# Five filter taps per chunk, as whole rows read from the transposed bank, with the running sum in SBUF

## The chip, the cores and the metric

The kernel runs on one core of a Trainium2 chip. The metric is the device time of one execution in microseconds; each kernel is run several times and the median is given.

## What is computed

Attention with a decay that depends on the position, then a gated unit whose gate is a causal filter over five positions. Eight batches, eight heads, 576 positions, 64 per head; the heads side by side make 512 features.

```python
def _attn_ref(q, k, v, s):
    scores = scale * np.matmul(q, k.transpose(0, 1, 3, 2))
    cum = np.cumsum(np.maximum(s, 0.0), axis=-1)
    bias = -(cum[:, :, :, None] - cum[:, :, None, :])
    scores = np.where(causal, -1000000000.0, scores + np.minimum(bias, 0.0))
    ...
    return np.matmul(attn, v)

def _moe_ref(x, w_val, conv_w, w_out):
    xp = np.concatenate([np.zeros((B, K - 1, D)), x], axis=1)
    for k in range(K):
        gate_pre += conv_w[k][None, None, :] * xp[:, k:k + S, :]
    gate = 1.0 / (1.0 + np.exp(-gate_pre))
    val = x @ w_val
    return (gate * val @ w_out)
```

## The kernel before

The work is cut into 32 chunks, `n = 4 * b + p`: batch `b` and a pair `p` of heads, which is also a chunk of 128 of the 512 features. One chunk passes through these steps; the engine stands in brackets.

- q and k are loaded (issued by SP), cast to bf16 (POOL), transposed into a PSUM bank (PE, L529) and copied to `QKT` (ACT, L533). v is loaded and multiplied with the decay (POOL, L500).
- The scores of two heads go in three steps to one of two double banks `s` (PE, L538; the causal mask is added by the matmuls of L580), and ACT takes their exponentials into `P` (L583, 128 x 1024 each, three a chunk).
- `av`: the weighted sum of v, with the sum of the weights as a 65th column, one bank per head (PE, L593).
- `norm`: per head, a reciprocal (DVE, L599) and a product that writes the normalised x in bf16 to `xn` (DVE, L600).
- `x_T`: x is transposed by five PE transposes into a bank of 576 bf16 (L607), and `x_evac` copies that bank to `xT` in SBUF behind four zero columns (DVE, L611).
- `tap`: the filter. The row of 576 is done in two halves of 288. The first product, with the fifth weight, goes to a PSUM bank `gs`; it is made by ACT (L623) for the chunks in `ON_ACT` (21 of 32) and by DVE (L625) for the other 11. Four more taps on DVE (L629) multiply a shifted piece of `xT` by a weight per partition and add what the bank holds; three write the bank again and the last writes the sum to `gp` in SBUF.
- `tanh`: ACT turns `gp` into `th` (L633); the sigmoid of the reference is half of one plus the tanh of half the argument.
- `val`: x times w_val, two halves a chunk, four matmuls each into a bank (PE, L653), after all four chunks of the batch are in `xT`. `glu` multiplies with one plus `th` (DVE, L659).
- `out`: five blocks a batch, four matmuls each (PE, L665), copied to `ot` by ACT (L670) and stored (SP).

At the end DVE looks at the reciprocals (L810 to L812); if one is out of range, a slower general path runs, which it does not here.

PSUM has eight banks: the two double banks `s` take four, and four single banks `m` are shared by everything else: the transposed q and k, the two `av` of a chunk, the transposed x, the `gs` halves, `val` and `out`. `gp` has two buffers, `th` six, `P` three.

The order of the work is not written by hand. `Plan` holds a list of tasks, each with an engine, an assumed duration, a due time, the tasks it needs, and the buffers that it takes and gives back. `Plan.run` plays them out in time: each engine takes the ready task with the smallest due time, and the order that results is the order in which each engine's instructions are issued on the chip. Each engine runs its own list strictly in that order, so an instruction that waits holds up everything behind it. The due times come from the table `DUE` (in chunks, added to the chunk's number).

Of the kernel before, what the change touches and what calls it, by code (L numbers as in the profile page):

```python
# [16 lines left out]
B, H, S, D = 8, 8, 576, 64  # L17
DM = 512
NKB = 5
# [184 lines left out]
def pcol(kb, qb):  # L204
    if kb == qb:
        return kb * 128
    if qb == 4:
# [13 lines left out]

DUE = dict(av=0.35, norm=0.78, xt=0.86, xe=-3.88, tap=1.56, dtap=0.01, tanh=0.36, cpe=-12.17, val=4.61,
           dval=0.23, out=9.61, dout=0.77, oute=-13.36, qt=-3.41, qe=-3.11, tt=-2.05, te=-14.54, s4=-1.53,
           vp=-12.15, cast=-20.65, lqk=-9.83, lv=17.78)

ON_PE = ()
PE_CHUNK = 2

ON_ACT = tuple(n for n in range(32) if n % 3)


class Plan:
# [115 lines left out]
def main_path(ctx, tc, q, k, v, s, moe_w_val, moe_conv_w, moe_w_out, out, okcnt):  # L350
# [5 lines left out]
    nc = tc.nc  # L356
# [49 lines left out]
    xns = two("xn", [128, NKB, 512], BF16)  # L406
    xTs = two("xT", [128, 4, 4 + S], BF16)
# [5 lines left out]
    recs = one.tile([128, NS, 2, NKB], FP32, name="recs")  # L413
# [3 lines left out]
    cwT = one.tile([128, 4, 5], FP32, name="cwT")  # L417
# [17 lines left out]
    def decay_T():  # L435
        pt = bank("w", [128, NKB, 64])
        slot["w"] = pt
        for i in range(NKB):
            nc.tensor.transpose(pt[:, i, :], cum[:, WIN[i]:WIN[i] + 128], identf)

    t = add("DVE", 0.65, -8, relu, [t_s])
    t = add("DVE", 1.3, -8, total, [t])
    t = add("DVE", 0.75, -8, centre, [t])
    t = add("PE", 1.2, -8, decay_T, [t], take=[("m", "w")], mode="N")
    t_w = add("ACT", 0.5, -8, lambda: nc.scalar.activation(out=w, in_=slot["w"], func=AF.Exp), [t],
              give=[("m", "w")])
# [3 lines left out]
    for nm, src, dst, sc, key in (("wv", moe_w_val, wv, 1.0, -5), ("wo", moe_w_out, wo, 0.5, -2.4)):  # L450
# [3 lines left out]
        t = add("SP", 3.6, key, load, take=[("qkf", nm)])  # L454
# [27 lines left out]
    T = {}  # L482
# [110 lines left out]
                nc.tensor.matmul(ps[:, qb * 65:qb * 65 + 65], lhsT, Vps[b % 2][:, kb, 2 * p + hh, :],  # L593
                                 start=(kb == 0), stop=(kb == qb))

    def norm(n, hh):
        b, p = divmod(n, 4)
        pv = slot["av", n, hh].rearrange("t (g d) -> t g d", d=65)
        nc.vector.reciprocal(recs[:, n, hh], pv[:, :, 64])  # L599
        nc.vector.tensor_tensor(xns[b % 2][:, :, p * 128 + hh * 64:p * 128 + hh * 64 + 64], pv[:, :, 0:64],  # L600
                                recs[:, n, hh].unsqueeze(2).to_broadcast([128, NKB, 64]), ALU.mult)

    def x_T(n):
        b, p = divmod(n, 4)
        pt = slot["x", n] = bank(("x", n), [128, S], BF16)
        for i in (4, 0, 1, 2, 3):
            nc.tensor.transpose(pt[:, WIN[i]:WIN[i] + 128], xns[b % 2][:, i, p * 128:(p + 1) * 128], ident)  # L607

# [1 line left out]
        b, p = divmod(n, 4)  # L610
        nc.vector.tensor_copy(xTs[b % 2][:, p, 4:4 + S], slot["x", n])  # L611

    def tap(n, hf, m):

        b, c = divmod(n, 4)
        o = hf * 288
        xc = xTs[b % 2][:, c, o:o + 292]
        if m == 0:
            slot["gs", n, hf] = bank(("gs", n, hf), [128, 288])
            if hf == 0:  # L620
                slot["g", n] = work("gp", n, [128, S], FP32)
            if n in ON_ACT:
                nc.scalar.activation(out=slot["gs", n, hf], in_=xc[:, 4:292], func=AF.Copy, scale=cwT[:, c, 4:5])  # L623
            else:
                nc.vector.tensor_scalar(slot["gs", n, hf], xc[:, 4:292], cwT[:, c, 4:5], None, ALU.mult)  # L625
        else:
            gs = slot["gs", n, hf]
            dst = slot["g", n][:, o:o + 288] if m == 4 else gs
            nc.vector.scalar_tensor_tensor(dst, xc[:, m - 1:m + 287], cwT[:, c, m - 1:m], gs, ALU.mult, ALU.add)  # L629

    def tanh(n):
        th = slot["t", n] = work("th", n, [128, S], FP32)
# [42 lines left out]
    for b in range(B):  # L675
# [3 lines left out]
        if b == 0:  # L679
            t_tl = add("SP", 1.6, -8.4, lambda: load_tail(0))  # L680
            t_tail = T["tailc", 0] = add("DVE", 0.45, -6, lambda: nc.vector.tensor_copy(tailbs[0], tails[0]), [t_tl])
            for p in range(4):
                for wh in range(2):
# [3 lines left out]
                    t = add("SP", 0.95, -8.5 + 0.5 * p + wh * 0.01, ld)  # L687
                    T["cast", 0, wh, p] = add(("DVE", "ACT")[wh], (0.32, 0.5)[wh], p - 9, lambda p=p, wh=wh: cast_qk(
                        (nc.vector.tensor_copy, nc.scalar.copy)[wh], 0, wh, HP[p], slot["f", 0, wh, p]), [t])
                t = add("SP", 1.4, -8.3 + 0.5 * p, lambda p=p: load_v_pair(p))  # L690
                T["vp", 0, p] = add("DVE", 0.85, p - 2, lambda p=p: vprime(nc.vector, 0, p), [t, t_w])
        else:
            fs = []
            for wh in range(2):
                def ld(b=b, wh=wh):
                    f = slot["f", b, wh] = work("qkf", (b, wh), [128, 8, 256], FP32)
                    dma_qk(b, wh, slice(0, 8), f)
                t = add("SP", 3.8, n0 + DUE["lqk"], ld, take=[("qkf", (b, wh))])
# [10 lines left out]
            for p in range(4):  # L709
# [3 lines left out]
        t = T["tt", b] = add("PE", 0.25, n0 + DUE["tt"] if b else -6.5, lambda b=b: tail_T(b), [t_tail],  # L713
                             take=[("m", ("tt", b))], mode="N")
# [19 lines left out]
        for p in range(4):  # L734
            n = n0 + p
            es = []
            for i in range(3):
                take = [("s", ("s", n, i))] + ([("P", n)] if i == 0 else [])
                t = T["s", n, i] = add("PE", (0.56, 0.27, 0.27)[i], n + 0.3 * i, lambda n=n, i=i: scores(n, i),
                                       [T["qe", b, p], t_te, T.get(("s", n, i - 1)), T.get(("s", n - 1, 2))],  # L740
                                       take=take, mode="R")
                es.append(add("ACT", 0.905, n + 0.3 * i, lambda n=n, i=i: exps(n, i), [t],
                              give=[("s", ("s", n, i))]))
            ns = []
            for hh in range(2):
# [3 lines left out]
                ns.append(add("DVE", 0.62, n + DUE["norm"] + 0.1 * hh, lambda n=n, hh=hh: norm(n, hh),  # L749
                              [t, T.get(("xt", n - 8))], give=[("m", ("av", n, hh))]))  # L750
            T["norm", n] = ns[1]
            t = T["xt", n] = add("PE", 0.3, n + DUE["xt"], lambda n=n: x_T(n), ns, take=[("m", ("x", n))], mode="N")

            T["xe", n] = add("DVE", 0.37, n + DUE["xe"], lambda n=n: x_evac(n),
                             [t] + [T.get(("val", n0 - 8 + c, hf)) for c in range(4) for hf in range(2)]
                             + T.get(("conv", n - 8), []), give=[("m", ("x", n))])
            ths = []
            if PE_CONV(b, p):
                cs = []
                for hf in range(2):  # L760
                    t = add("PE", 1.85, n + DUE["cpe"], lambda n=n, hf=hf: conv_pe(n, hf), [T["xe", n], t_dg] + cs[-1:],
                            take=[("m", ("g", n, hf))], mode="N")
                    cs.append(t)
                    ths.append(add("ACT", 0.42, n + DUE["cpe"] + 0.2, lambda n=n, hf=hf: tanh_pe(n, hf), [t] + ths,
                                   take=[("th", n)] if hf == 0 else [], give=[("m", ("g", n, hf))]))
                T["conv", n] = cs
            else:
                ends = []
                for hf in range(2):
                    t = ends[0] if hf else None  # L770
                    for m in range(5):
                        take = [("gp", n)] if m + hf == 0 else []
                        if m == 0:
                            take = take + [("m", ("gs", n, hf))]
                        t = add("ACT" if m == 0 and n in ON_ACT else "DVE", 0.37, n + DUE["tap"] + (hf * 2.5 + m * 0.5) * DUE["dtap"],
                                lambda n=n, hf=hf, m=m: tap(n, hf, m), [T["xe", n], t_cw, t], take=take,
                                give=[("m", ("gs", n, hf))] if m == 4 else [])
                    ends.append(t)
                T["conv", n] = ends
# [102 lines left out]
```

## Time and profile before

| what | value |
|---|---|
| median of 3 runs | 270.92 us (270.29 to 271.18) |
| the profiled execution | 271.83 us |
| its span in the trace | 270.0 us |
| mean granted TensorE clock | 0.938 |
| busy: PE, DVE, ACT, POOL | 197.8, 226.0, 194.9, 73.3 us |
| DMA: moved, mean rate | 40.5 MB, 150 GB/s |

A group of instructions is written as its line, engine and operation, what it writes and reads by the program's names (buffer numbers left out), then partitions x elements and type, and after the bar the busy time in us, the mean duration of one in ns, the idle time of the engine just before such instructions and what ended it. So `L629 DVE ... m<-xT,cwT,m 128x288` is a tap of half a row. A row of the waits names who waited, for whom, the total in us, how often, and the longest. The 40 slices give the busy share in tenths. PE's busy time is that of overlapping matmuls and says less of how full PE is than it does for DVE and ACT.

### The profile page before, as it was taken

What the parts mean: (1) busy time and instruction counts of PE and PEld (TensorE: products, weight loads), DVE (VectorE), ACT (ScalarE), POOL (GpSimd) and SP (SyncE); (2) the same over time, 40 slices, a digit from 0 to 9 for tenths busy, and PEclk for the clock granted to TensorE, in tenths of its full rate; (3) what the DMA queues carried; (4) which work ended last, traced back from release to release, by engine and by line L of the source; (5) the groups of instructions that cost most, each with busy time, mean ns of one, the idle gap of its engine ahead of it and who ended that gap; (6) DMA issues with size and microseconds to landing.
All of it is one profiled execution on the core that took longest, in us unless ns stands there. A gap on an engine that the chain in (4) does not pass through costs nothing. (4 is left out here: it accounts for less than half of the span.)

```text
span 270.0 us, 6360 instructions
## 1 busy us (share of the span) xinstructions
PE 197.8 (73%) x2539; PEld 127.8 (47%) x2561; DVE 226.0 (84%) x524; ACT 194.9 (72%) x267; POOL 73.3 (27%) x73
## 2 busy tenths in 40 slices
PE   0788776766598679876849886887878776986660
PEld 0465642554456445553436553555445544543420
DVE  4453699899999898999987998999899999999920
ACT  2789788434888989878865787977987797684330
POOL 9204236457022810300930057042033000000000
PEclk9999965688889999999967999999999999999998
DMA  6999999989259970794421910752560120043133
GB/s 168 258 297 304 179 264 300 195 230 328 62 187 227 311 233 23 165 261 142 162 71 26 224 68 2 168 107 80 122 114 37 53 89 2 2 155 136 42 104 105
DMA packets 69232, 40.50 MB, mean 150 GB/s; under 512 B 47109, under 2 KB 63493, under 8 KB 69194
## 3 DMA queue, kind: packets, MB, share of 16 engines
q1 hardware_dynamic: 69194, 40.01, 56.7%
q8 instruction: 22, 0.36, 0.6%
q14 instruction: 16, 0.13, 0.2%
HBM read 30.57 MB, written 9.44 MB: 148 GB/s over the span
## 5 line engine op out<-in xcount | busy, mean ns | idle before, releaser
L583 ACT ACTIVATE P<-s 128x1024 bf16<-128x1024 f32 x96 | 95.1, 1027 | 14.4 <-PE s L580 9.5
L629 DVE SCALAR_TENSOR_TENSOR m<-xT,cwT,m 128x288 f32<-128x288 bf16 x192 | 99.6, 521 | 6.3 <-ACT m L623 1.6
L653 PE MATMUL m<-xT,wv 128*128 128x288 bf16 x256 | 43.6, 309 | 10.1 <-DVE gp L629 8.5
L538 PE MATMUL s<-QKT 64*128 64x128 bf16 (+4 forms) x576 | 41.4, 253 | 13.0 <-ACT P L583 10.6
L593 PE MATMUL m<-Vp,P 128*128 128x65 bf16 x960 | 40.8, 199 | 10.1 <-DVE gp L629 7.4
L500 POOL TENSOR_TENSOR Vp<-vst,w 128x650 bf16<-128x650 f32 x28 | 35.1, 1283 | 42.2 <-DMA vst<-in_v_dram 36.7
L665 PE MATMUL m<-wo,glu 128*128 128x512 bf16 x138 | 39.5, 384 | 9.5 <-DVE gp L629 7.3
L593 PEld LDWEIGHTS <-P 128*128 128x128 bf16 x960 | 36.4, 101 | 19.2 <-DVE gp L629 8.0
L538 PEld LDWEIGHTS <-QKT 64*128 64x128 bf16 x576 | 21.6, 99 | 34.0 <-issue 26.3
L533 ACT COPY QKT<-m 128x1024 bf16<-128x1024 bf16 x32 | 32.2, 1017 | 6.5 <-PE m L529 6.3
L653 PEld LDWEIGHTS <-wv 128*128 128x128 bf16 x256 | 24.6, 103 | 23.3 <-issue 13.6
L629 DVE SCALAR_TENSOR_TENSOR gp<-xT,cwT,m 128x288 f32<-128x288 bf16 x64 | 32.8, 514 | 2.1
L633 ACT ACTIVATE th<-gp 128x576 f32<-128x576 f32 x32 | 21.9, 684 | 15.9 <-DVE gp L629 15.6
L600 DVE TENSOR_TENSOR xn<-m,recs 128x320 bf16<-128x320 f32 x64 | 31.5, 492 | 2.2
L623 ACT ACTIVATE m<-xT,cwT 128x288 f32<-128x288 bf16 x42 | 21.1, 506 | 15.9 <-DVE glu L659 5.8
L670 ACT COPY ot<-m 128x512 f32<-128x512 f32 (+1 forms) x40 | 23.3, 584 | 11.9 <-PE m L665 9.4
L659 DVE SCALAR_TENSOR_TENSOR glu<-th,m 128x288 bf16<-128x288 f32 x64 | 26.7, 448 | 1.8 <-PE m L653 1.5
L665 PEld LDWEIGHTS <-glu 128*128 128x128 bf16 x160 | 14.4, 98 | 22.8 <-issue 7.5
L490 POOL CAST qb<-qkf 128x2048 bf16<-128x2048 f32 x7 | 13.3, 1894 | 37.1 <-issue 22.4
L529 PE MATMUL m<-ident,qb 128*128 128x128 bf16 x128 | 13.1, 227 | 12.0 <-DVE chalf L432 6.4
L607 PE MATMUL m<-ident,xn 128*128 128x128 bf16 x160 | 14.8, 225 | 6.4 <-DVE xn L600 5.1
L611 DVE COPY xT<-m 128x576 bf16<-128x576 bf16 x32 | 14.5, 452 | 4.4 <-PE m L607 4.3
(59 smaller groups left out, 160.2 us busy)
## 6 DMA issues: line engine op xcount, KB each, us to landing
out_dram<-ot SPq DMA_DIRECT2D x32, 256.0 KB, 2.1
qkf<-in_q_dram SPq DMA_DIRECT2D x7, 1024.0 KB, 5.9
qkf<-in_k_dram SPq DMA_DIRECT2D x7, 1024.0 KB, 7.9
vst<-in_v_dram SPq DMA_DIRECT2D x28, 256.0 KB, 5.0
vst<-in_v_dram SPq DMA_DIRECT2D x15, 128.0 KB, 4.3
first<-in_q_dram SPq DMA_DIRECT2D x4, 256.0 KB, 3.5
first<-in_k_dram SPq DMA_DIRECT2D x4, 256.0 KB, 3.6
tail<-in_q_dram SPq DMA_DIRECT2D x8, 128.0 KB, 8.8
```

What stands on the lines that cost most here:

```text
L500: eng.tensor_tensor(Vps[b % 2][:, :, h], vst[:, :, h], w[:, :, b * 8 + 2 * p:b * 8 + 2 * p + 2].unsqueeze(3).to_broadcast([128, NKB, 2, 65 ...
L533: nc.scalar.copy(QKTs[b % 2][:, :, p, 0:512].rearrange("d w (x j) -> d w x j", j=4), slot["qt", b, p].rearrange("d w (j x) -> d w x j", j=4))
L538: nc.tensor.matmul(ps[:, hh, c0:c0 + nq], QKTs[b % 2][r, 1, p, k0:k0 + 128], QKTs[b % 2][r, 0, p, q0:q0 + nq], **kw)
L583: nc.scalar.activation(out=slot["Pt", n][:, :, step * 512:(step + 1) * 512], in_=slot["s", n, step], func=AF.Exp, scale=0.125)
L593: nc.tensor.matmul(ps[:, qb * 65:qb * 65 + 65], lhsT, Vps[b % 2][:, kb, 2 * p + hh, :], start=(kb == 0), stop=(kb == qb))
L600: nc.vector.tensor_tensor(xns[b % 2][:, :, p * 128 + hh * 64:p * 128 + hh * 64 + 64], pv[:, :, 0:64], recs[:, n, hh].unsqueeze(2).to_broad ...
L629: nc.vector.scalar_tensor_tensor(dst, xc[:, m - 1:m + 287], cwT[:, c, m - 1:m], gs, ALU.mult, ALU.add)
L633: nc.scalar.activation(out=th, in_=slot["g", n], func=AF.Tanh, scale=0.5)
L653: nc.tensor.matmul(ps, wv[:, dc, c * 128:(c + 1) * 128], xTs[b % 2][:, dc, 4 + o:4 + o + 288], start=(dc == 0), stop=(dc == 3))
L659: nc.vector.scalar_tensor_tensor(glus[b % 2][:, c, o], slot["t", n][:, o], 1.0, slot["v", n, hf], ALU.add, ALU.mult)
L665: nc.tensor.matmul(ps, glus[b % 2][:, c, WIN[i]:WIN[i] + 128], wo[:, c, :], start=(c == 0), stop=(c == 3))
L670: nc.scalar.copy(ot[r, :], slot["o", b, i][r, :])
```

## The change

- A chunk's taps run over the whole row of 576 instead of two halves. They read x from the PSUM bank into which it was transposed, not from `xT`. The shift by one to four positions is made by shortening: tap `sh` reads `x[:, 0:576 - sh]` and adds to `gp[:, sh:576]`, so the zero columns are not needed for it.
- The running sum stays in `gp` in SBUF from the first product to the last tap; the `gs` banks are gone.
- `x_evac` still copies x to `xT`, for `val`, and the first product comes after it. The bank of x is given back after the fourth tap, no longer after the copy. `gp` is taken by `x_T`, no longer by the first product.
- The first product is on ACT for the 16 odd chunks and on DVE for the 16 even ones.
- `norm` is one task for both heads: two reciprocals, then two products. It waits for both `av`.
- The assumed durations of these tasks and most entries of `DUE` differ, so the order moves on every engine.

```diff
-DUE = dict(av=0.35, norm=0.78, xt=0.86, xe=-3.88, tap=1.56, dtap=0.01, tanh=0.36, cpe=-12.17, val=4.61,
+DUE = dict(av=0.17, norm=-1.06, xt=0.72, xe=0.23, tap=1.91, dtap=0.12, tanh=-1.57, cpe=-14.16, val=4.61,
...
-           vp=-12.15, cast=-20.65, lqk=-9.83, lv=17.78)
+           vp=-14.19, cast=-23.73, lqk=-8.62, lv=14.96)
...
-ON_ACT = tuple(n for n in range(32) if n % 3)
+ON_ACT = tuple(range(1, 32, 2))
...
-    def norm(n, hh):
+    def norm(n):
         b, p = divmod(n, 4)
...
+        pvs = [slot["av", n, hh].rearrange("t (g d) -> t g d", d=65) for hh in range(2)]
+        for hh in range(2):
+            nc.vector.reciprocal(recs[:, n, hh], pvs[hh][:, :, 64])
+        for hh in range(2):
+            nc.vector.tensor_tensor(xns[b % 2][:, :, p * 128 + hh * 64:p * 128 + hh * 64 + 64], pvs[hh][:, :, 0:64],
+                                    recs[:, n, hh].unsqueeze(2).to_broadcast([128, NKB, 64]), ALU.mult)
...
         pt = slot["x", n] = bank(("x", n), [128, S], BF16)
+        if not PE_CONV(b, p):
+            slot["g", n] = work("gp", n, [128, S], FP32)
...
-    def tap(n, hf, m):
+    def tap(n, m):
...
+        x, gp = slot["x", n], slot["g", n]
+        sh = (4 - (m - 1)) % 5 if m else 0
         if m == 0:
...
             if n in ON_ACT:
-                nc.scalar.activation(out=slot["gs", n, hf], in_=xc[:, 4:292], func=AF.Copy, scale=cwT[:, c, 4:5])
+                nc.scalar.activation(out=gp, in_=x, func=AF.Copy, scale=cwT[:, c, 4:5])
             else:
-                nc.vector.tensor_scalar(slot["gs", n, hf], xc[:, 4:292], cwT[:, c, 4:5], None, ALU.mult)
+                nc.vector.tensor_scalar(gp, x, cwT[:, c, 4:5], None, ALU.mult)
         else:
...
+            nc.vector.scalar_tensor_tensor(gp[:, sh:S], x[:, 0:S - sh], cwT[:, c, 4 - sh:5 - sh], gp[:, sh:S],
+                                           ALU.mult, ALU.add)
...
+            ns = [add("DVE", 1.1, n + DUE["norm"], lambda n=n: norm(n), [t, T.get(("xt", n - 8))],
+                      give=[("m", ("av", n, hh)) for hh in range(2)])]
...
+            t = T["xt", n] = add("PE", 0.3, n + DUE["xt"], lambda n=n: x_T(n), ns,
+                                 take=[("m", ("x", n))] + ([] if on_pe else [("gp", n)]), mode="N")
...
+                t = T["xe", n]
+                for m in range(5):
+                    act = m == 0 and n in ON_ACT
+                    t = add("ACT" if act else "DVE", 0.54 if act else 0.67, n + DUE["tap"] + m * DUE["dtap"],
+                            lambda n=n, m=m: tap(n, m), [t_cw, t], give=[("m", ("x", n))] if m == 4 else [])
+                T["conv", n] = [t]
```

Two places in the order. The first is DVE in the middle of the program, at a chunk whose first product DVE makes. Names carry a number for each tile: `m_2650` is one use of a shared bank, `gp_2651` one use of a sum buffer, and x2 or x3 counts equal rows that follow each other. Before, with `m_2650` and `m_2692` the two halves of one chunk:

```order
239 L625 TENSOR_SCALAR m_2650<-xT_118,cwT 128x288
240 L629 SCALAR_TENSOR_TENSOR m_2650<-xT_118,cwT,m_2650 128x288 x3
241 L629 SCALAR_TENSOR_TENSOR gp_2651<-xT_118,cwT,m_2650 128x288
242 L611 COPY xT_118<-m_2678 128x576
243 L625 TENSOR_SCALAR m_2692<-xT_118,cwT 128x288
244 L629 SCALAR_TENSOR_TENSOR m_2692<-xT_118,cwT,m_2692 128x288 x3
245 L629 SCALAR_TENSOR_TENSOR gp_2651<-xT_118,cwT,m_2692 128x288
```

And now, at such a chunk of the changed kernel, where `m_2452` is the bank of x, with the norm that follows:

```order
226 L615 COPY xT_118<-m_2452 128x576
227 L626 TENSOR_SCALAR gp_2453<-m_2452,cwT 128x576
228 L628 SCALAR_TENSOR_TENSOR gp_2453<-m_2452,cwT,gp_2453 128x572
229 L628 SCALAR_TENSOR_TENSOR gp_2453<-m_2452,cwT,gp_2453 128x573
230 L628 SCALAR_TENSOR_TENSOR gp_2453<-m_2452,cwT,gp_2453 128x574
231 L628 SCALAR_TENSOR_TENSOR gp_2453<-m_2452,cwT,gp_2453 128x575
232 L600 RECIPROCAL recs<-m_2494 128x5
233 L600 RECIPROCAL recs<-m_2527 128x5
234 L602 TENSOR_TENSOR xn_116<-m_2494,recs 128x5x64
235 L602 TENSOR_TENSOR xn_116<-m_2527,recs 128x5x64
```

Ten instructions of half a row have become five of a row, the source is the bank of x itself, and the taps follow directly on the copy of that bank; the norm's two reciprocals stand together.

The second place is ACT, also in the middle, around first products and tanh. Before:

```order
121 L623 ACTIVATE m_2052<-xT_119,cwT 128x288
122 L583 ACTIVATE P_1998<-s_2014 128x2x512
123 L633 ACTIVATE th_2070<-gp_1936 128x576
124 L533 COPY QKT_112<-m_2043 128x2x512
125 L623 ACTIVATE m_2091<-xT_119,cwT 128x288
126 L583 ACTIVATE P_1998<-s_2056 128x2x512
```

And now:

```order
121 L633 ACTIVATE th_2088<-gp_1981 128x576
122 L533 COPY QKT_113<-m_2090 128x2x512
123 L624 ACTIVATE gp_2082<-m_2081,cwT 128x576
124 L583 ACTIVATE P_2107<-s_2106 128x2x512
125 L583 ACTIVATE P_2107<-s_2121 128x2x512
126 L583 ACTIVATE P_2107<-s_2135 128x2x512
127 L633 ACTIVATE th_2164<-gp_2082 128x576
```

Two half products per chunk, each with its own place in ACT's list, have become one whole product that reads the bank of x and writes the sum buffer; the three exponentials of the next scores stand behind it and ahead of its tanh.

More of the change, by code (lines that the diff above doesn't have):

```diff
@@ L220 @@
 NEG = -30000.0
-DUE = dict(av=0.35, norm=0.78, xt=0.86, xe=-3.88, tap=1.56, dtap=0.01, tanh=0.36, cpe=-12.17, val=4.61,
-           dval=0.23, out=9.61, dout=0.77, oute=-13.36, qt=-3.41, qe=-3.11, tt=-2.05, te=-14.54, s4=-1.53,
-           vp=-12.15, cast=-20.65, lqk=-9.83, lv=17.78)
+DUE = dict(av=0.17, norm=-1.06, xt=0.72, xe=0.23, tap=1.91, dtap=0.12, tanh=-1.57, cpe=-14.16, val=4.61,
+           dval=0.42, out=9.65, dout=0.73, oute=-18.67, qt=-4.54, qe=-7.61, tt=-1.92, te=-14.48, s4=-1.31,
+           vp=-14.19, cast=-23.73, lqk=-8.62, lv=14.96)
 ON_PE = ()
 PE_CHUNK = 2
-ON_ACT = tuple(n for n in range(32) if n % 3)
+ON_ACT = tuple(range(1, 32, 2))
 class Plan:
@@ L594, in av @@
                                  start=(kb == 0), stop=(kb == qb))
-    def norm(n, hh):
+    def norm(n):
         b, p = divmod(n, 4)
[L598 to L601, printed above, removed]
+        pvs = [slot["av", n, hh].rearrange("t (g d) -> t g d", d=65) for hh in range(2)]
[4 more added lines that the diff above has]
+                                    recs[:, n, hh].unsqueeze(2).to_broadcast([128, NKB, 64]), ALU.mult)
     def x_T(n):
@@ L611, in x_evac @@
         nc.vector.tensor_copy(xTs[b % 2][:, p, 4:4 + S], slot["x", n])
-    def tap(n, hf, m):
+    def tap(n, m):
         b, c = divmod(n, 4)
-        o = hf * 288
-        xc = xTs[b % 2][:, c, o:o + 292]
+        x, gp = slot["x", n], slot["g", n]
+        sh = (4 - (m - 1)) % 5 if m else 0
         if m == 0:
-            slot["gs", n, hf] = bank(("gs", n, hf), [128, 288])
-            if hf == 0:
-                slot["g", n] = work("gp", n, [128, S], FP32)
             if n in ON_ACT:
-                nc.scalar.activation(out=slot["gs", n, hf], in_=xc[:, 4:292], func=AF.Copy, scale=cwT[:, c, 4:5])
+                nc.scalar.activation(out=gp, in_=x, func=AF.Copy, scale=cwT[:, c, 4:5])
             else:
-                nc.vector.tensor_scalar(slot["gs", n, hf], xc[:, 4:292], cwT[:, c, 4:5], None, ALU.mult)
+                nc.vector.tensor_scalar(gp, x, cwT[:, c, 4:5], None, ALU.mult)
         else:
-            gs = slot["gs", n, hf]
-            dst = slot["g", n][:, o:o + 288] if m == 4 else gs
-            nc.vector.scalar_tensor_tensor(dst, xc[:, m - 1:m + 287], cwT[:, c, m - 1:m], gs, ALU.mult, ALU.add)
+            nc.vector.scalar_tensor_tensor(gp[:, sh:S], x[:, 0:S - sh], cwT[:, c, 4 - sh:5 - sh], gp[:, sh:S],
+                                           ALU.mult, ALU.add)
     def tanh(n):
@@ L748, in main_path @@
                                         give=[("P", n)] if hh else [], mode="N")
[L749 to L752, printed above, removed]
+            ns = [add("DVE", 1.1, n + DUE["norm"], lambda n=n: norm(n), [t, T.get(("xt", n - 8))],
+                      give=[("m", ("av", n, hh)) for hh in range(2)])]
+            T["norm", n] = ns[0]
+            on_pe = PE_CONV(b, p)
+            t = T["xt", n] = add("PE", 0.3, n + DUE["xt"], lambda n=n: x_T(n), ns,
+                                 take=[("m", ("x", n))] + ([] if on_pe else [("gp", n)]), mode="N")
             T["xe", n] = add("DVE", 0.37, n + DUE["xe"], lambda n=n: x_evac(n),
                              [t] + [T.get(("val", n0 - 8 + c, hf)) for c in range(4) for hf in range(2)]
-                             + T.get(("conv", n - 8), []), give=[("m", ("x", n))])
+                             + T.get(("conv", n - 8), []), give=[("m", ("x", n))] if on_pe else [])
             ths = []
@@ L767, in main_path @@
             else:
[L768 to L779, printed above, removed]
+                t = T["xe", n]
[4 more added lines that the diff above has]
+                T["conv", n] = [t]
                 ths = [add("ACT", 0.59, n + DUE["tanh"], lambda n=n: tanh(n), [t], take=[("th", n)], give=[("gp", n)])]
```

## The prediction

> **What bounds the kernel now.** I read the page's list of busy times and its 40 slices first, then the table of stretches, then the groups of instructions, then who waited for whom, last the timeline of DVE near the end. The list of busy times alone does not settle it: DVE leads, but PE and ACT are not far behind.
>
> ```profile
> PE 197.8 (73%) x2539; PEld 127.8 (47%) x2561; DVE 226.0 (84%) x524; ACT 194.9 (72%) x267; POOL 73.3 (27%) x73
> DVE  4453699899999898999987998999899999999920
> ```
>
> The slices show why 84% is too low a figure for DVE: the first four are half empty (loads and the first scores), the last two are empty (the last stores), and between them almost every slice is at 8 or 9 tenths. The table of stretches puts numbers to it; its columns are the stretch, its length, and the busy time of PE, of the weight loads, of DVE, ACT and POOL.
>
> ```profile
> 30.00:60.00 30.00, 21.11 (x258) 13.96 (x256) 26.70 (x57) 20.54 (x27) 13.79 (x12) 0.70 0.97 233
> 60.00:90.00 30.00, 23.49 (x289) 15.85 (x290) 27.78 (x66) 21.95 (x31) 10.93 (x8) 0.90 0.82 213
> 90.00:120.00 30.00, 23.31 (x338) 15.10 (x343) 28.10 (x67) 26.18 (x35) 8.22 (x7) 1.00 0.72 187
> 120.00:150.00 30.00, 22.21 (x284) 14.26 (x280) 26.31 (x61) 21.82 (x30) 8.70 (x6) 0.89 0.37 114
> 150.00:180.00 30.00, 24.00 (x323) 15.31 (x328) 27.77 (x67) 25.07 (x35) 10.10 (x8) 1.00 0.51 108
> 180.00:210.00 30.00, 24.27 (x338) 15.91 (x341) 28.28 (x68) 23.37 (x33) 9.21 (x8) 1.00 0.36 89
> 210.00:240.00 30.00, 24.18 (x322) 14.89 (x325) 28.78 (x71) 24.20 (x35) 0.00 (x0) 1.00 0.15 54
> 240.00:258.00 18.00, 11.75 (x92) 6.73 (x95) 17.19 (x40) 7.93 (x14) 0.00 (x0) 1.00 0.28 96
> ```
>
> From 30 to 258 us, 228 us in all, DVE is busy 210.9 us (the sum of its column): 92.5%. Its lowest stretch is 26.31 of 30, 88%. The 32 chunks take 228 / 32 = 7.1 us each in this body. Who waited says the same from the other side: what ACT and PE wait for is mostly DVE's taps.
>
> ```profile
> ACT th L633 <- DVE gp L629: 15.6, 23, 2.6
> PE m L653 <- DVE gp L629: 8.5, 10, 1.7
> PE m L593 <- DVE gp L629: 7.4, 10, 1.5
> PE m L665 <- DVE gp L629: 7.3, 8, 1.4
> ```
>
> The tanh waits 15.6 us for the sums, and PE waits 8.5 + 7.4 + 7.3 = 23.2 us, in L653, L593 and L665, for a bank that a last tap frees. So DVE's work in the body is what the time is made of, and the costliest part of that work is what the change rewrites.
>
> **The taps.** These groups carry the terms: elements per partition, count, then busy us and mean ns of one.
>
> ```profile
> L629 DVE SCALAR_TENSOR_TENSOR m<-xT,cwT,m 128x288 f32<-128x288 bf16 x192 | 99.6, 521 | 6.3 <-ACT m L623 1.6
> L629 DVE SCALAR_TENSOR_TENSOR gp<-xT,cwT,m 128x288 f32<-128x288 bf16 x64 | 32.8, 514 | 2.1
> L625 DVE TENSOR_SCALAR m<-xT,cwT 128x288 f32<-128x288 bf16 x22 | 11.4, 517 | 0.6
> L659 DVE SCALAR_TENSOR_TENSOR glu<-th,m 128x288 bf16<-128x288 f32 x64 | 26.7, 448 | 1.8 <-PE m L653 1.5
> L811 DVE SCALAR_TENSOR_TENSOR ok<-recs,ok 128x320 f32<-128x320 f32 x1 | 0.5, 492 | 0.0
> L500 DVE TENSOR_TENSOR Vp<-vst,w 128x650 bf16<-128x650 f32 x4 | 3.3, 833 | 4.1 <-DMA vst<-in_v_dram 2.9 <-ACT w L445 1.2
> L600 DVE TENSOR_TENSOR xn<-m,recs 128x320 bf16<-128x320 f32 x64 | 31.5, 492 | 2.2
> L611 DVE COPY xT<-m 128x576 bf16<-128x576 bf16 x32 | 14.5, 452 | 4.4 <-PE m L607 4.3
> ```
>
> An element's price on DVE, from two rows of one operation: (833 - 492) / (650 - 320) = 1.03 ns. Of the 514 ns of a tap of 288, about 297 are elements and 217 are paid however short the row is. The change makes 128 taps of 572 to 575 elements out of 256 of 288 (in the order of DVE, a chunk's ten instructions become five), so half of those fixed parts go. A new tap is 514 + 286 x 1.03 = 809 ns. No row shows one that reads PSUM, adds to SBUF and writes SBUF, so I bound it: from below by the gate product, which reads one operand in PSUM and one in SBUF and writes SBUF, 448 + 286 x 1.03 = 743 ns; from above by no saving at all, 2 x 521 = 1042 ns. I take 809, since the tap that already writes gp is the same operation with the same kind of scalar. A first product on DVE becomes 517 + 288 x 1.03 = 814 ns; its ends are 452 (the copy of x, the same bank read in the same length) and 2 x 517 = 1034.
>
> The source moves from SBUF to PSUM. The rows give no price to that: the gate product with an operand in PSUM takes 448 ns for 288 elements, the all-SBUF product of L811 492 for 320, which is 492 - 32 x 1.03 = 459 for 288. [...] I stay with the rows, in which PSUM is not the dearer source.
>
> What an instruction occupies is not its duration. The timeline of DVE, start and duration in us:
>
> ```profile
> 240.92 0.52 DVE L625 TENSOR_SCALAR m<-xT,cwT 128x288 f32<-128x288 bf16 x1
> 241.48 1.64 DVE L629 SCALAR_TENSOR_TENSOR m<-xT,cwT,m 128x288 f32<-128x288 bf16 x3
> 243.15 0.52 DVE L629 SCALAR_TENSOR_TENSOR gp<-xT,cwT,m 128x288 f32<-128x288 bf16 x1
> 243.58 0.19 DVE L599 RECIPROCAL recs<-m 128x5 f32<-128x5 f32 x1
> 243.81 0.49 DVE L600 TENSOR_TENSOR xn<-m,recs 128x320 bf16<-128x320 f32 x1
> 244.21 1.63 DVE L629 SCALAR_TENSOR_TENSOR m<-xT,cwT,m 128x288 f32<-128x288 bf16 x3
> ```
>
> Three dependent taps take 243.15 - 241.48 = 1.67 us, 0.557 each, 0.034 more than a duration; the last one, followed by unrelated work, gives way after 0.43, 0.085 before its end. Half a chunk is 2.10 us (241.48 to 243.58), with its first product on DVE 2.66. Before, 21 chunks cost 4.20 and 11 cost 5.32: a mean of 4.59 us. After, four dependent taps cost 3 x 0.843 + 0.724 = 3.25, with the first product 0.848 more; 16 chunks each: a mean of 3.68. Saved: 0.91 us a chunk.
>
> **The norm.** A reciprocal and its product take 0.63 us (243.58 to 244.21), 1.26 a chunk; the product starts 0.23 after the reciprocal, which it needs. With both reciprocals first, the second fills that gap: 0.23 + 0.40 + 0.40 = 1.03. The saving lies between nothing and 0.23; I take 0.2. Both now wait for the second half's AV matmuls, and behind them on DVE stand the copy of x and the taps; the cover is DVE's own queue of taps, and if it runs dry the wait is one AV, 0.61 us in a row of PE quoted below, which eats the saving.
>
> Together 0.91 + 0.2 = 1.1 us a chunk, 35 us over 32 chunks. With the ends of the tap: 1.36 + 0 to 0.23 at 743 ns, about nothing at 1042.
>
> **ScalarE.** The first product of fewer chunks, over a whole row:
>
> ```profile
> L623 ACT ACTIVATE m<-xT,cwT 128x288 f32<-128x288 bf16 x42 | 21.1, 506 | 15.9 <-DVE glu L659 5.8 <-DVE xT L611 4.7 <-DVE gp L629 2.6
> L583 ACT ACTIVATE P<-s 128x1024 bf16<-128x1024 f32 x96 | 95.1, 1027 | 14.4 <-PE s L580 9.5 <-PE s L538 4.8
> L558 ACT ACTIVATE P<-s 128x128 bf16<-128x128 f32 x4 | 1.2, 294 | 0.4 <-PE s L553 0.4
> L633 ACT ACTIVATE th<-gp 128x576 f32<-128x576 f32 x32 | 21.9, 684 | 15.9 <-DVE gp L629 15.6
> ```
>
> An element costs (1027 - 294) / 896 = 0.82 ns, so a row of 576 is 506 + 288 x 0.82 = 742 ns, with the tanh's 684 below and 2 x 506 = 1012 above. ACT goes from 21.1 to 16 x 0.742 = 11.9 us: 9 us less, 0.3 a chunk. It hides under DVE now and matters only where ACT becomes the longest.
>
> **What is late next.** In the table, 30 us hold 30 / 7.1 = 4.2 chunks: 4.6 us off DVE, 1.2 off ACT, nothing off PE. The longest engine of each stretch is then DVE 22.1, PE 23.5, ACT 25.0, PE 22.2, PE 24.0, PE 24.3, PE or DVE 24.2, and in the last, with 2.5 chunks, DVE 14.4: together 179.7 us. Divided by the share that this engine reaches, it gives the new body. DVE reached 92.5%, as the one bound; with three engines within some 2 us in most stretches each waits for the others more often, and I take the lowest share of any stretch, 88%: 204 us, 24 less than 228. The profiled execution took 271.8 us (span 270.0); 271.8 - 24 = 248. It lies 0.9 above the median of the runs, 270.9, so I forecast **247 us**. Head and tail I leave as they are: DVE is not what is late there.
>
> The due times also shift the loads on SP's queue against the chunks (q and k by 1.2 chunks, v by 2.8) and the casts on POOL. POOL is idle most of the span and gets no more work; the stretch from 30 to 60 is the one where the transfers stand at 0.97. If it does not shrink at all, it keeps 30 us where I count 22.1 / 0.88 = 25.1: 5 us, a result of 252, inside the forecast.
>
> **Rivals.** *DVE stays the one bound, at 92.5%.* 179.7 / 0.925 = 194, 34 us less: 237. For it: the freed waits of ACT and PE are waits for DVE. Against it: ACT's 25.0 and PE's 24 beside it. 17%, 234 to 241.
>
> *The long row saves little,* or the new waits take most of it. At 1042 ns DVE is left as it was, and a few us remain, 268; with the body at 82%, 219, it is 9 us, 262. For it: no row shows this operand mix. Against it: the fixed 217 ns in three rows. 15%, 257 to 269.
>
> *Slower: banks.* x stays in its bank from the transposition to the fourth tap, some 5 us alone and up to two chunks' DVE work when others come between; and x_T now also needs a gp buffer, so it stands at PE's head until the tanh two chunks earlier is over. With the AV, val, out and q/k matmuls queued behind it on PE, ACT's exponentials run out. Two x at once leave 2 of 4 banks for the rest. What those hold, from the timeline of PE and two groups of ACT:
>
> ```profile
> 201.77 0.65 PE L653 MATMUL m<-xT,wv 128*128 128x288 bf16 x4
> 202.26 0.61 PE L593 MATMUL m<-Vp,P 128*128 128x65 bf16 x15
> ...
> 208.59 1.03 PE L665 MATMUL m<-wo,glu 128*128 128x512 bf16 x4
> ...
> 211.58 0.40 PE L529 MATMUL m<-ident,qb 128*128 128x128 bf16 x4
> 211.81 0.39 PE L529 MATMUL m<-ident,kb 128*128 128x128 bf16 x4
> ```
> ```profile
> L533 ACT COPY QKT<-m 128x1024 bf16<-128x1024 bf16 x32 | 32.2, 1017 | 6.5 <-PE m L529 6.3
> L670 ACT COPY ot<-m 128x512 f32<-128x512 f32 x32 | 18.6, 585 | 8.1 <-PE m L665 7.1 <-DMA out_dram<-ot 0.8
> ```
>
> Per chunk, waits left out, I estimate two AV banks of about 1.9 us (two AV, a reciprocal, one or two products of 0.49), two val banks of 0.65 + 0.45, one q/k bank of 0.62 + 1.02, and 1.25 out banks of 1.03 + 0.59: 3.8 + 2.2 + 1.6 + 2.0 = 9.6 us, 4.8 on two banks. It decides when queueing lengthens that by half, to 7.25 us a chunk, 0.15 over today's 7.1: 32 x 0.15 = 5 us, 276. For it: PE's 23 us of waits for banks. Against it: the two half-row banks go, 2 x 2.1 us or more a chunk. [...] 9%.
>
> *No change,* the two effects balancing: 4%.
>
> **The numbers.** Forecast 55%, 242 to 256; the rivals as said. About 0.3%, 0.8 us, is what a measurement of this kernel can tell from no change. Faster 55 + 17 + 15 = 87%, same 4%, slower 9%. The range of 8 in 10 takes the forecast, most of the first rival and a half of the second: 235 to 261.
>
> **What would show it.** Taps of 572 to 575 elements near 0.81 us, 128 of them, 104 us where 132 stood; DVE busy near 190; first products on ACT near 0.74; DVE's share of the body below 92%, with PE or ACT at its side; PE's waits for a bank, freed by a tap, not above 23 us. I am wrong if a tap takes over 0.95 us, or if PE's waits grow past 50.

## The result, and the profile after

| | before | after |
|---|---|---|
| median | 271.05 us | 239.80 us (4 runs, 239.30 to 241.54) |
| ratio, with its 95% interval | | 0.886 (0.881 to 0.891) |
| span of the profiled execution | 270.0 us | 237.6 us |

A few executions of a kernel fall into a slower state, and every median here is that of the others. The changed kernel is 31 us faster. The forecast was 247 us, 24 faster. The measured time lies in the range, but outside the forecast's own case (242 to 256) and inside that of the first rival (234 to 241). The page of after, busy times and DVE's slices:

```profile
PE 190.1 (80%) x2561; PEld 124.4 (52%) x2561; DVE 193.1 (81%) x390; ACT 184.9 (78%) x241; POOL 73.5 (31%) x73
DVE  4435599999999796998784996999999999999800
```

DVE lost 226.0 - 193.1 = 32.9 us, the span 32.4. The same table of stretches as before; the body now ends at 227 us, with DVE's last instruction (its last gate product ends at 225.4):

```profile
30.00:60.00 30.00, 22.10 (x316) 15.31 (x317) 29.31 (x52) 24.52 (x30) 14.82 (x14) 0.94 0.96 250
60.00:90.00 30.00, 27.53 (x419) 18.63 (x418) 27.77 (x60) 29.45 (x39) 19.13 (x13) 1.00 0.96 261
90.00:120.00 30.00, 24.45 (x320) 16.77 (x318) 25.02 (x51) 22.92 (x31) 9.31 (x7) 0.94 0.79 212
120.00:150.00 30.00, 24.29 (x359) 16.13 (x359) 23.80 (x50) 23.44 (x31) 9.30 (x7) 1.00 0.33 85
150.00:180.00 30.00, 27.84 (x387) 18.30 (x386) 29.16 (x61) 27.12 (x36) 8.83 (x8) 1.00 0.61 130
180.00:210.00 30.00, 27.63 (x383) 17.20 (x382) 29.12 (x61) 26.75 (x35) 1.17 (x1) 1.00 0.14 50
210.00:227.00 17.00, 14.34 (x109) 8.00 (x107) 14.79 (x30) 7.58 (x13) 0.00 (x0) 1.00 0.32 117
```

Three of the stretches have DVE at 97% or more (29.1 to 29.3 of 30) and one has ACT at 98% (29.45). Of the stretches of 30 us, only the two in the middle, 90 to 150 us, have no engine above 25.0. DVE as a whole is busy 179.0 of the body's 197 us, 90.8%; the longest engine of each stretch, summed, 181.1: 91.9%.

The groups of the tap, of its first products and of the norm, in mean ns:

```profile
L628 DVE SCALAR_TENSOR_TENSOR gp<-m,cwT,gp 128x575 f32<-128x575 bf16 x32 | 26.0, 814 | 0.6
L628 DVE SCALAR_TENSOR_TENSOR gp<-m,cwT,gp 128x572 f32<-128x572 bf16 x32 | 25.9, 810 | 3.2 <-ACT gp L624 2.8
L626 DVE TENSOR_SCALAR gp<-m,cwT 128x576 f32<-128x576 bf16 x16 | 13.0, 810 | 0.0
L624 ACT ACTIVATE gp<-m,cwT 128x576 f32<-128x576 bf16 x16 | 12.1, 756 | 5.3 <-DVE xT L615 2.8 <-DVE cwT L478 2.4
L600 DVE RECIPROCAL recs<-m 128x5 f32<-128x5 f32 x64 | 9.2, 176 | 11.0 <-PE m L593 11.0
```

A tap takes 810 to 814 ns, where 809 was worked out; a first product 810 on DVE (814) and 756 on ACT (742). The timeline of DVE shows what they occupy:

```profile
207.75 0.81 DVE L628 SCALAR_TENSOR_TENSOR gp<-m,cwT,gp 128x572 f32<-128x572 bf16 x1
208.47 0.26 DVE L600 RECIPROCAL recs<-m 128x5 f32<-128x5 f32 x2
208.70 0.89 DVE L602 TENSOR_TENSOR xn<-m,recs 128x320 bf16<-128x320 f32 x2
209.50 1.66 DVE L628 SCALAR_TENSOR_TENSOR gp<-m,cwT,gp 128x573 f32<-128x573 bf16 x2
211.07 0.45 DVE L615 COPY xT<-m 128x576 bf16<-128x576 bf16 x1
```

The norm takes 209.50 - 208.47 = 1.03 us, as estimated (it is also the median of the 32 chunks); the tap ahead of it gives way after 0.72; two dependent taps take 1.57 until the copy. The waits:

```profile
DVE recs L600 <- PE m L593: 11.0, 14, 2.3
ACT th L633 <- DVE gp L628: 6.6, 10, 1.4
PE m L653 <- DVE glu L659: 5.5, 8, 1.3
DVE gp L628 <- ACT gp L624: 2.8, 5, 1.7
DVE xT L615 <- PE m L611: 2.6, 5, 0.8
PE m L529 <- DVE gp L628: 2.4, 3, 1.3
PE m L593 <- DVE gp L628: 1.2, 3, 0.6
PE m L665 <- DVE gp L628: 1.0, 2, 0.6
PE m L653 <- DVE gp L628: 0.8, 1, 0.8
```

The tanh's wait for the sums went from 15.6 to 6.6 us, and PE's waits for a bank that a tap frees, in L653, L593 and L665, from 23.2 to 3.0; the row of 2.4 in L529 was 3.1 before. Two waits grew: the norm's for AV on DVE, from 5.8 to 11.0 us, now that its reciprocals come behind both heads, and PE's in L653 for a gate product, from 0.5 to 5.5.

### The profile page after: what moved, and what is told of

Same layout as the page of the kernel before. It is cut to its first block, busy times and chain, and to the rows that moved or that the text cites. A ratio compares the mean times of both kernels' runs of the same rounds, so it can differ in the third digit from the quotient of the medians.

```text
span 237.6 us, 6221 instructions
## 1 busy us (share of the span) xinstructions
PE 190.1 (80%) x2561; PEld 124.4 (52%) x2561; DVE 193.1 (81%) x390; ACT 184.9 (78%) x241; POOL 73.5 (31%) x73
## 5 line engine op out<-in xcount | busy, mean ns | idle before, releaser
L628 DVE SCALAR_TENSOR_TENSOR gp<-m,cwT,gp 128x572 f32<-128x572 bf16 (+3 forms) x128 | 103.7, 812 | 5.1 <-ACT gp L624 2.8
L538 PE MATMUL s<-QKT 64*128 64x128 bf16 (+4 forms) x576 | 40.6, 247 | 10.0 <-ACT P L583 7.4
L653 PE MATMUL m<-xT,wv 128*128 128x288 bf16 x256 | 40.5, 293 | 7.7 <-DVE glu L659 5.5
L593 PE MATMUL m<-Vp,P 128*128 128x65 bf16 x960 | 39.3, 197 | 4.4 <-DVE gp L628 1.2
L665 PE MATMUL m<-wo,glu 128*128 128x512 bf16 x160 | 40.2, 380 | 2.2 <-DVE gp L628 1.0
L593 PEld LDWEIGHTS <-P 128*128 128x128 bf16 x960 | 35.0, 100 | 12.6 <-issue 3.6
L538 PEld LDWEIGHTS <-QKT 64*128 64x128 bf16 x576 | 20.6, 96 | 27.6 <-issue 18.9
L653 PEld LDWEIGHTS <-wv 128*128 128x128 bf16 x256 | 24.1, 99 | 20.6 <-issue 12.7
L659 DVE SCALAR_TENSOR_TENSOR glu<-th,m 128x288 bf16<-128x288 f32 x64 | 27.8, 448 | 5.1 <-PE m L653 4.8
L602 DVE TENSOR_TENSOR xn<-m,recs 128x320 bf16<-128x320 f32 x64 | 28.1, 481 | 0.0
L665 PEld LDWEIGHTS <-glu 128*128 128x128 bf16 x160 | 14.2, 98 | 15.5 <-issue 3.6
L529 PE MATMUL m<-ident,qb 128*128 128x128 bf16 x128 | 13.1, 228 | 11.3 <-DVE chalf L432 6.1
L600 DVE RECIPROCAL recs<-m 128x5 f32<-128x5 f32 x64 | 9.2, 176 | 11.0 <-PE m L593 11.0
L529 PEld LDWEIGHTS <-qb 128*128 128x128 bf16 x128 | 8.7, 101 | 16.6 <-issue 7.7
```

The source lines that it names most:

```text
L538: nc.tensor.matmul(ps[:, hh, c0:c0 + nq], QKTs[b % 2][r, 1, p, k0:k0 + 128], QKTs[b % 2][r, 0, p, q0:q0 + nq], **kw)
L628: nc.vector.scalar_tensor_tensor(gp[:, sh:S], x[:, 0:S - sh], cwT[:, c, 4 - sh:5 - sh], gp[:, sh:S], ALU.mult, ALU.add)
L653: nc.tensor.matmul(ps, wv[:, dc, c * 128:(c + 1) * 128], xTs[b % 2][:, dc, 4 + o:4 + o + 288], start=(dc == 0), stop=(dc == 3))
L659: nc.vector.scalar_tensor_tensor(glus[b % 2][:, c, o], slot["t", n][:, o], 1.0, slot["v", n, hf], ALU.add, ALU.mult)
L665: nc.tensor.matmul(ps, glus[b % 2][:, c, WIN[i]:WIN[i] + 128], wo[:, c, :], start=(c == 0), stop=(c == 3))
```

## The experiments

Each differs from the changed kernel by the edit shown, unless it says otherwise. The times are medians; the changed kernel stands at 239.8, the kernel before at 271.05 to 271.4 beside the various runs.

**The source of the taps.** `e1_src_sbuf_hold`:

```diff
-        x, gp = slot["x", n], slot["g", n]
+        x, gp = xTs[b % 2][:, c, 4:4 + S], slot["g", n]
+        if m == 4:
+            x = slot["x", n]
```

> The first product and three of the four taps read the copy of x in SBUF; the last tap still reads the bank, so the bank is held as long as in the changed kernel, and the order is the same. If the source has no price, as the rows of before say: taps of 0.81 us from either memory, 240 us within 1. [...]

Measured: 265.6 us, 26 slower than the changed kernel (ratio to the kernel before 0.977, 0.974 to 0.981). The expectation does not hold. The lines of the taps in this run, minimum, median and longest in ns; then DVE and POOL by time:

```profile
L630 DVE SCALAR_TENSOR_TENSOR gp<-xT,cwT,gp x96: 799/815/2324, 31.5 to 246.1; 128x572 f32<-128x572 bf16 x32, 128x573 f32<-128x573 bf16 x32, 128x574 f32<-128x574 bf16 x32
L630 DVE SCALAR_TENSOR_TENSOR gp<-m,cwT,gp x32: 803/816/818, 34.1 to 246.9; 128x575 f32<-128x575 bf16 x32
```
```profile
121.04 1.66 DVE L630 SCALAR_TENSOR_TENSOR gp<-xT,cwT,gp 128x573 f32<-128x573 bf16 x2
123.64 0.80 DVE L630 SCALAR_TENSOR_TENSOR gp<-m,cwT,gp 128x575 f32<-128x575 bf16 x1
127.81 5.82 DVE L630 SCALAR_TENSOR_TENSOR gp<-xT,cwT,gp 128x572 f32<-128x572 bf16 x3
134.57 0.81 DVE L630 SCALAR_TENSOR_TENSOR gp<-m,cwT,gp 128x575 f32<-128x575 bf16 x1
```
```profile
125.57 1.89 POOL L490 CAST qb<-qkf 128x2048 bf16<-128x2048 f32 x1 [4.34 <-issue]
127.41 2.12 POOL L490 CAST kb<-qkf 128x2048 bf16<-128x2048 f32 x1
129.49 6.52 POOL L500 TENSOR_TENSOR Vp<-vst,w 128x650 bf16<-128x650 f32 x4
```

Most taps take 0.81 us from either memory. But a tap with both operands in SBUF that meets a cast or a product of POOL takes up to 2.3 us: from 127.4 to 136 us POOL works, and three taps with xT and gp in SBUF take 5.82 us together. Of the 96, the 31 that overlap such a POOL instruction take 1.49 us in the mean and the other 65 take 0.811. The tap that reads the bank never takes more than 0.818, here as in the changed kernel. POOL is held up as well: its products take 1.51 us instead of 1.28. DVE's busy time rises to 214.0 us, 21 above after. So the source does matter, in a way that the prediction did not have: beside a cast or product of POOL, the taps with both operands in SBUF took 1.49 us, and those with x in the bank 0.818 at most.

The first products on DVE, which have a single tensor operand, were changed in e1 too, and their line shows something else that nobody expected:

```profile
L628 DVE TENSOR_SCALAR gp<-xT,cwT x16: 510/562/1600, 30.7 to 238.2; 128x576 f32<-128x576 bf16 x16
```

The eight of them that meet nothing of POOL take 0.52 us, where they take 0.81 from the bank; the eight that meet POOL take up to 1.60. For this instruction SBUF is the cheaper source, by 0.29 us, when POOL is idle.

`e2_src_sbuf_free` leaves out the lines `if m == 4` as well, so all four taps have both operands in SBUF.

> As e1, but the last tap reads SBUF too, so the bank of x is free once it is copied, in the same order of instructions. If holding the bank through the taps costs anything: faster than e1, by up to the 5 us that PE waits for taps in the changed kernel. If banks are not what PE lacks: the same as e1 within 1 us.

Measured: 268.7 us, 3 slower than e1, where the same or less was expected, with a fourth tap exposed. Freeing the bank earlier in the same order bought nothing that shows beside that; it could not be parted from the source here.

`e10_pool_writes`, from e2: from the second batch on POOL no longer reads v, q and k. The kernel leaves out the scaled v and the casts and writes constants of the same shapes in their place.

```diff
-        eng.tensor_tensor(Vps[b % 2][:, :, h], vst[:, :, h],
...
+        if b:
+            for i in range(2):
+                eng.memset(Vps[b % 2][:, :, h], 1.0)
+            return
...
+        if b:
+            nc.gpsimd.memset(qkbs[which][b % 2][:, :, :], 0.25)
+            return
```

> As e2 (taps read SBUF twice), but from the second batch on POOL only writes constants of the same shapes into Vp, qb and kb, instead of reading v, q and k; the scaled v and the casts are left out. If POOL's reads of SBUF are what holds up a tap with two SBUF operands: taps that meet POOL take 0.81 us as the others do, no tap above 0.9, and the time falls from 270 to 241 or less. If a second SBUF operand is dear by itself, or POOL's writes hold it up too: taps of 1.4 us where they meet POOL, 260 or more.

Measured: 242.8 us, 26 faster than e2, with the same DVE instructions and POOL busy as long as in the changed kernel (73.2 us). The taps:

```profile
L635 DVE SCALAR_TENSOR_TENSOR gp<-xT,cwT,gp x128: 803/814/1146, 31.0 to 224.8; 128x572 f32<-128x572 bf16 x32, 128x573 f32<-128x573 bf16 x32, 128x574 f32<-128x574 bf16 x32, 128x575 f32<-128x575 bf16 x32
L633 DVE TENSOR_SCALAR gp<-xT,cwT x16: 512/520/2002, 30.4 to 216.1; 128x576 f32<-128x576 bf16 x16
```

The long taps are gone. Only three of 128 are above 0.83 us, up to 1.15, and each of them meets a cast of the tail, the one thing that POOL still reads for. So what held up the taps in e1, 1.49 us against 0.811, went with POOL's reads: here, with the same two SBUF operands and POOL writing, the median is 0.814 and no tap is long beside a POOL instruction that only writes. The first products (second line) behave otherwise: four of the 16 take 1.07 to 2.00 us, and each of these meets a constant that POOL writes, so for these four writing alone was enough. That is 5 us of DVE over the undisturbed 0.52 each, and the time lies 2 us above the 241 that was expected.

In e10 the bank of x is given back as early as in e2, and it still is 3 us slower than the changed kernel. So no gain from freeing the bank early shows here either, though the long first products cost some of it.

**Halves.** `e3_halves`:

```diff
-            nc.vector.scalar_tensor_tensor(gp[:, sh:S], x[:, 0:S - sh], cwT[:, c, 4 - sh:5 - sh], gp[:, sh:S],
-                                           ALU.mult, ALU.add)
+            for o, e in ((sh, 288), (288, S)):
+                nc.vector.scalar_tensor_tensor(gp[:, o:e], x[:, o - sh:e - sh], cwT[:, c, 4 - sh:5 - sh], gp[:, o:e],
+                                               ALU.mult, ALU.add)
...
+                for o in (0, 288):
+                    nc.vector.tensor_scalar(gp[:, o:o + 288], x[:, o:o + 288], cwT[:, c, 4:5], None, ALU.mult)
```

> Every tap and first product of DVE is cut into two halves again, still from the bank and with the sum in SBUF, in the same places of the order. Leaves nothing out. If each instruction simply pays its fixed 217 ns again: 8 x 0.557 against 3.25 us of taps a chunk, 1.2 us a chunk more, up to 38 us, near 275. If most of that is the wait of a tap for the one that it needs, which two halves taken in turn hide from each other: 8 x 0.43 = 3.44 us a chunk, 0.2 more, 6 us, 246.

Measured: 249.9 us (0.921, 0.916 to 0.926), 10 slower than whole rows. DVE is busy 205.2 us, 12 more, in this line of its page:

```profile
PE 191.5 (77%) x2561; PEld 125.1 (50%) x2561; DVE 205.2 (83%) x534; ACT 185.7 (75%) x241; POOL 74.2 (30%) x73
```

Far from 38 and nearer to 6: two halves taken in turn hide from each other the wait of a tap for the one that it needs. In the trace of e3 a half tap makes room for the next after 0.424 us (from start to start), against 0.557 for the dependent half taps of the kernel before; eight take 3.39 us a chunk. In the changed kernel 58 of the 128 taps have another tap right behind them and make room after 0.84 us, the other 70 have other work behind them and make room after 0.73: 3.13 us a chunk. The difference, 0.26 a chunk, is 8 of the 10 us. So whole rows are worth 10 us in this order, not the whole gain.

**The order.** `e4_old_due` puts the due times of before into the changed kernel:

```diff
-DUE = dict(av=0.17, norm=-1.06, xt=0.72, xe=0.23, tap=1.91, dtap=0.12, tanh=-1.57, cpe=-14.16, val=4.61,
+DUE = dict(av=0.35, norm=0.78, xt=0.86, xe=-3.88, tap=1.56, dtap=0.01, tanh=0.36, cpe=-12.17, val=4.61,
...
```

> The changed kernel with the due times of the kernel before, so the same instructions in another order. If the gain is DVE's lighter load and DVE stays the one bound: within 4 us of 240. If the new order is what let it come out at the high share of 92% (the forecast had taken 88%): back to the forecast's 247 or above.

Measured: 267.7 us (0.984, 0.979 to 0.990): only 3.6 us faster than before. DVE's instructions are those of the changed kernel (their durations add up to 215 us in both; fewer overlap here, so the busy time is 197.8 us and not 193.1), but it stands idle between them. Its page and waits:

```profile
PE 200.3 (75%) x2561; PEld 132.1 (50%) x2561; DVE 197.8 (74%) x390; ACT 186.5 (70%) x241; POOL 73.2 (28%) x73
```
```profile
ACT th L633 <- DVE gp L628: 21.3, 16, 3.2
...
DVE xT L615 <- PE m L611: 16.3, 21, 1.8
...
DVE gp L628 <- ACT gp L624: 12.2, 12, 2.3
...
PE m L653 <- DVE gp L628: 8.2, 5, 3.0
...
PE m L665 <- DVE gp L628: 7.4, 8, 2.1
```

The copy of x waits 16.3 us for its transposition (2.6 in the changed kernel), a tap 12.2 for ACT's first product (2.8), and PE 8.2 + 7.4 us for banks of x in L653 and L665 alone. From 30 to 254 us DVE is busy 183.8 of 224, 82%; the longest engine of each stretch, summed, gives 84%.

`e9_before_new_due` is the other half: the kernel before, with the new due times.

> The kernel before with the due times of the changed kernel, so that only the order moves. If that order is better in itself: below 265. If an order fits the durations and banks that it was chosen for, as e4 suggests from the other side: 271 or slower.

Measured: 269.6 us (0.993, 0.990 to 0.996), between the two expectations and near the second. The new order alone is worth 0.7%, and DVE stays busy 206.3 of the 224 us from 30 to 254, 92%. So the new instructions alone give 3.6 us, the new order alone about 1.9, and both together 31: the lighter DVE needs an order that feeds it. Which of the due times does it is not shown; they were only changed all together.

**What bounds now.** Three doses of work that nobody needs, each on one engine:

```diff
+            if m == 4:
+                nc.vector.tensor_reduce(pad[:, 0, 0:1], w.rearrange("p a b -> p (a b)"), AX.X, ALU.min)
```
```diff
         nc.scalar.activation(out=th, in_=slot["g", n], func=AF.Tanh, scale=0.5)
+        nc.scalar.copy(pad, w)
```
```diff
+        if hf == 0:
+            for dc in range(3):
+                nc.tensor.matmul(ps, wv[:, dc, c * 128:(c + 1) * 128], xTs[b % 2][:, dc, 4 + o:4 + o + 288],
+                                 start=(dc == 0), stop=(dc == 2))
```

> The changed kernel with one more DVE instruction per chunk, a reduction of 320 elements that nobody needs, behind the last tap, in the same order: by the row of such a reduction (0.486 us, some 0.40 until the next) 32 x 0.40 = 13 us of DVE. If DVE is still the one bound (the first rival of the prediction): 12 to 14 us more, 253. If PE and ACT share the bound (the forecast): about half of it, 246.

> The changed kernel with one more ACT instruction per chunk, a copy of 320 elements behind the tanh that nobody needs, some 0.37 us until the next: 12 us of ACT. If DVE is the one bound: 3 us or less, 243. If three engines share it: about half, 246.

> The changed kernel with three more matmuls per chunk ahead of the first val half, whose sum is overwritten: 3 x 0.12 x 32 = 12 us of PE. If DVE is the one bound: 3 us or less, 243. If three engines share it: about half, 246.

Measured: 248.8, 245.4 and 241.2 us. The busy lines, DVE's dose first, then ACT's, then PE's:

```profile
PE 192.7 (78%) x2561; PEld 125.0 (51%) x2561; DVE 207.0 (84%) x422; ACT 185.7 (75%) x241; POOL 74.1 (30%) x73
```
```profile
PE 191.1 (79%) x2561; PEld 125.6 (52%) x2561; DVE 194.0 (80%) x390; ACT 194.7 (80%) x273; POOL 74.9 (31%) x73
```
```profile
PE 199.7 (84%) x2657; PEld 134.1 (56%) x2657; DVE 194.0 (81%) x390; ACT 185.1 (77%) x241; POOL 73.3 (31%) x73
```

By busy time, 13.9 us more on DVE cost 9.0 us, 9.8 more on ACT 5.6, and 9.6 more on PE 1.4: 0.65, 0.57 and 0.15 us per us. DVE and ACT share the bound about evenly. PE, with 190 us busy, hardly belongs to it: its 1.4 us are not clear of the noise (240.3 to 243.4 us, against 239.3 to 241.5 without the dose). Each dose was given at one place of the order, so these are the prices at that place. So the first rival's time came out, but not its mechanism: DVE is not the one bound.

**The norm.** `e8_norm_apart`:

```diff
         for hh in range(2):
             nc.vector.reciprocal(recs[:, n, hh], pvs[hh][:, :, 64])
-        for hh in range(2):
...
```

> The norm as reciprocal, product, reciprocal, product again, still behind both AV and in the same place of the order. The prediction gave the pairing 0.2 us a chunk, 6 us in all: 246 if DVE is the bound and the pairing is worth that, 240 if the gap between a reciprocal and its product was worth nothing.

Measured: 243.7 us (0.897, 0.893 to 0.901), 3.9 slower. DVE's busy time rises by 5.9 us, to 199.0, which is 0.18 us a chunk: the estimate of 0.2 holds, and two thirds of it reach the end.

**More first products on ACT.** `e11_act_21` and `e12_act_all`:

```diff
-ON_ACT = tuple(range(1, 32, 2))
+ON_ACT = tuple(n for n in range(32) if n % 3)
```
```diff
-ON_ACT = tuple(range(1, 32, 2))
+ON_ACT = tuple(range(32))
```

> The changed kernel with the first product on ACT for 21 chunks, as before, instead of 16: 5 x 0.85 = 4 us off DVE, 5 x 0.66 = 3 us more on ACT. At the 0.65 us per us that e5 measured for DVE and 0.57 for ACT: 1 us faster, 239; if ACT's list is held up by waits for the copy of x: 242 or more.

> The first product on ACT for all 32 chunks: 13.6 us off DVE, 10.6 more on ACT. By the same two slopes 8.8 less and 6.0 more, 237; if ACT becomes the one bound and its waits for the copy of x grow: 245.

Measured: 243.6 and 247.7 us; the expected gain is not there. With all on ACT, DVE is down to 183.7 us, but its taps wait for ACT, which is up to 194.3:

```profile
PE 190.0 (77%) x2540; PEld 126.8 (52%) x2561; DVE 183.7 (75%) x374; ACT 194.3 (79%) x257; POOL 75.1 (31%) x73
```
```profile
DVE gp L628 <- ACT gp L624: 11.5, 12, 1.6
```

The due times were not chosen anew for these two, so they say that this order wants the split at half, not that no order could use more of ACT. No run beat the changed kernel.

## Why the prediction was right in its sign and short in its size

**What bounds before**: right as far as the runs tell, but not enough. DVE is at 92% of the body in the kernel before in either order (92.5%, and 92% in e9), and its busy time and the span fell by nearly the same, 32.9 and 32.4 us. That equality proves little: in e4 DVE's busy time is 28.2 us lower than before and the time only 3.6. No dose was given to the kernel before, so how much of its bound DVE was is not measured.

**The tap, the first products, the norm**: right within 2% (809 for 810 to 814 ns, 814 for 810, 742 for 756, 1.03 us for 1.03). e8 confirms the pairing's 0.2 us a chunk. The taps' sum is 103.7 us by the group of the page of after (104 was named).

**The source has no price**: right for the taps, but for an incomplete reason, and wrong for the first products. Where it meets nothing of POOL a tap takes 0.811 us from SBUF (e1), and 0.812 from PSUM in the mean of all (the changed kernel). Reading the copy in SBUF instead of the bank cost 26 to 29 us here (e1, e2): with the sum in SBUF, a tap that reads the bank took 0.818 us at most, and one that reads the copy 1.49 in the mean beside a cast or product of POOL. The kernel before had it the other way round, x in SBUF and the sum in PSUM, and its taps were not held up either (0.524 us at most). A first product on DVE does pay for the bank, with 0.81 us against 0.52 where POOL is idle; over the 16 that is 4.6 us of DVE. No run reads the bank for the taps and the copy for the first products, so whether that would be faster stays open.

**The late part: "I take the lowest share of any stretch, 88%".** This is the step that failed. The sum of the longest engines came out (179.7 us forecast, 181.1 measured), in part by chance: PE was to be the longest in four of the eight stretches, and in the measured seven it is in one, with DVE in five. But the sum was divided by 0.88, and the body came out at 0.92: 197 us, not 204, and that is the 7 us between 247 and 239.8. Two things were wrong in it. PE was counted as a third bound at its busy time; e7 shows 0.15 us per us. And the share was taken for a matter of how many engines are near each other, while e4 shows that the order sets it: with the due times of before the same work runs at 84%, 267.7 us. The prediction gave the new order no price of its own; the 82% and 262 us that it named for its second rival are nearer to what it would have met without the new order than its own 88%.

**The bank rival**: not in the changed kernel, where PE's waits for taps fell instead of growing. In e4, PE waits 15.6 us in L653 and L665 for taps, about as long as before in these two lines (15.8), so with the old order the cost stays, and it does not grow as the rival had it: 268 us, not 276.

## What to carry to other kernels

In a kernel like this one, in which every engine runs a fixed list, a lighter engine may give its time back only if the order is remade for it: here the new instructions alone gave 3.6 us, the new order alone 1.9, and both 31. Where DVE and POOL work at once, count the SBUF operands of a DVE instruction that adds two tensors: here the kernels whose taps read the copy took 265.6 and 268.7 us against 239.8 with x in the bank, and giving the bank back early showed no gain (e2, e10). Test for the bound with a known dose of useless work on each engine; here the busy shares put PE level with DVE and ACT (80, 81 and 78%), the doses did not (0.15 us per us against 0.65 and 0.57).

## What the runs showed of the hardware that was not expected

- A DVE tap of 572 to 574 elements with both tensor operands in SBUF took 1.49 us in the mean where a cast or product of POOL overlapped it, and 0.811 where none did; POOL's product went from 1.28 to 1.51 us (e1). With POOL only writing, the taps' median was 0.814, and the only three above 0.83 met a cast that still read (e10).
- A first product on DVE, 576 elements of bf16 times a scalar to fp32 in SBUF, took 0.81 us from a PSUM bank (the changed kernel) and 0.52 from SBUF where it met nothing of POOL (e1). From SBUF it was held up by POOL, to 1.60 us in e1 and to 2.00 in e10, there also by POOL instructions that only write.
- A half tap made room after 0.557 us for a tap that needs its result (before), and after 0.424 for one that does not (e3). By the prediction's estimate of 1.03 ns an element its 288 elements are 0.297, so about half of the remaining 0.26 is the wait for the instruction ahead.
